# A three-part fp32 network on one core: the sequence transform folded a second time, its sums taken after the output projection, and the layer norm of two blocks inverted by token

## The chip, the cores and the metric

The kernel runs on one core of one Trainium2 chip. The metric is device time in microseconds; lower is better. A core has five engines with queues of their own: TensorE (PE in the views, with its weight loads, LDWEIGHTS, shown apart as PEld), VectorE (DVE), ScalarE (ACT), GpSimd (POOL) and SyncE (SP), which here issues DMAs.

## The reference

Three blocks follow one another, on 8 batches of 576 tokens with 512 features.

```python
# attention with random features, 8 heads of 64
q_p, k_p = phi(q), phi(k)          # phi: x @ w_phi, minus the row's largest |.|, exp(+) and exp(-)
num = q_p @ (k_p^T v);  den = q_p . sum(k_p) + 1e-6;  x = num / den
# gated mixer: 5 causal taps along the sequence
gate = sigmoid(sum_k conv_w[k] * x shifted by 4-k)
x = (gate * (x @ w_val)) @ w_out
# Fourier mixer and MLP
mixed = real(fft(fft(x, axis=sequence), axis=features))
u = x + mixed
un = (u - mean(u)) / sqrt(var(u) + 1e-6)
out = u + relu(un @ w_ch1) @ w_ch2
```

## The kernel before

**Numbers.** All products of the mixer, the transforms and the MLP are in fp32 split in two: a high part (copied to the fp32r type, on ACT: `o_hi`) and the rest (`o_lo`, on DVE or POOL), and three matmuls, high x high, high x low, low x high (`mm3`). The Fourier transforms are products with tables of cosines and sines.

**Stages.** Attention runs in 48 hand-written steps. Then a "mix" stage does, for each batch b, these parts, each written as a list of operations: `note_x` (load x, split it into `xh`), `note_taps` (the gate, sums in `acc`), `note_V` (value projection `val<-xh,wv`, 12 matmuls for each of 4 feature chunks and 2 halves of the sequence; the gate's product; the split `ge`), `note_W` (output projection `ps<-ge,wo`, also 8 times 12 matmuls; results in `x2`, which the trace calls x), `note_FD` (transform over features, `ps<-ft,f`, results `Y` and the rest `rem`), `note_SD` (transform over the sequence, `ps<-sq,Y` and `ps<-sr,rem`, and the sum `u`, stored to DRAM). Between them stand the first two half blocks of the layer norm (`ln_first`) and sums of MLP weights on POOL (`note_sums`). The MLP follows, in five blocks of tokens, with seven products where eight would be plain.

**Folding.** A real sequence has a transform that is symmetric, so one works on sums and differences of token s and token 576 - s. Before, these are taken of the gated value, ahead of W (`gs<-gv,val`): halves of 290 columns (289 tokens and one that overlaps) go through W as an even and an odd part, a = 0 and 1. The features are folded in the same way by the order of `w_out`'s columns and by `fs` (c and c - 2). In SD the results of 290 columns are added to x2, and `u` is made of its even and odd part, forwards and, read backwards, for the other half of the sequence. Feature 256 goes its own way, on single rows: `xr` into FD, `c256`, `r256`, and a product with 97 weight columns at the end of each four batches.

**Order.** After the parts are noted, `place_ops` sets the order of every engine in one list. It has a cost for each operation (by engine and columns), works backwards from the end to a due time for each, shifts some due times by a table of hand-made numbers (`MOVES`, operation number: half microseconds), and then lets each engine take the ready operation that is due first. An operation marked "vp" goes to DVE or POOL, whichever the list finds sooner. Engines then run in that order and wait by semaphores. `MOVES` and the noted order of V and W in `note_mix` are what the change touches here.

Nearly all instructions of this stage stand in the trace at one line (64 before, 66 after), that of a helper that issues them, so groups go by the names of their tiles.

## Time and profile before

| | |
|---|---|
| median of three runs | 1301.6 us (1301.53 to 1302.43) |
| profiled execution | 1302.1 us, span 1300.3 us |
| TensorE busy | 1281.4 us, 99% of the span |
| DVE, ACT, POOL busy | 1130.3, 917.2, 786.9 us |
| granted TensorE clock, mean | 0.999 of full speed |

The attention takes about the first 300 us of the span, the mix stage lies from there to about 585, the MLP from about 585 to 1296. Busy time counts instructions at work; a busy TensorE may still be at a lower clock, which the column PEclk of the windows shows as a share of full speed.

### The profile page before, as it was taken

The page shows a single profiled execution, that of the slowest core. Times are in us where ns is not written, and L with a number is a line of the kernel's source. Part 1 is how long each engine was busy: PE and PEld are TensorE (multiplying, and loading weights), DVE is VectorE, ACT ScalarE, POOL GpSimd, SP SyncE. Part 2 cuts the span into 40 slices and gives each one's busy share as a digit, 9 for nine tenths or more (in the row PEclk, how much of TensorE's full clock was granted, in tenths as well). Part 3 has the DMA queues.
Part 4 walks back from the last instruction along what each step waited for, and adds up shares of the span by engine and source line. Part 5 has one row for each costly group of instructions (what it writes and reads, how often), then busy time and mean ns, then how long its engine had stood idle before and what let it go on. Part 6 is the DMA issues. An engine that isn't in the chain of part 4 may idle for free.

```text
span 1300.3 us, 30757 instructions
## 1 busy us (share of the span) xinstructions
PE 1281.4 (99%) x11952; PEld 1181.0 (91%) x11952; DVE 1130.3 (87%) x1773; ACT 917.2 (71%) x1719; POOL 786.9 (61%) x660
## 2 busy tenths in 40 slices
PE   8999999999999999999999999999999999999998
PEld 7899999998999999998888888888888888899997
DVE  6888888888999999698889988898989898888785
...
GB/s 309 200 289 319 326 298 289 172 120 96 118 187 138 139 160 130 170 60 295 111 99 100 276 104 104 104 185 197 105 100 134 245 107 103 102 165 162 109 82 90
DMA packets 147005, 214.62 MB, mean 165 GB/s; under 512 B 18854, under 2 KB 105382, under 8 KB 146860
## 3 DMA queue, kind: packets, MB, share of 16 engines
...
HBM read 165.63 MB, written 46.99 MB: 164 GB/s over the span
## 4 chain that ended last, share of the span: by engine, by line
PE 86%; ACT 5%; DMA 4%; DVE 4%; issue 0%; POOL 0%; SPq 0%; POOLq 0%; DVEq 0%; ACTq 0%
PE x L64 15%; PE cx L64 15%; PE cy L64 11%; PE ps L64 11%; PE y L64 8%; PE val L64 7%; PE kv L64 5%; PE pj L64 4%; PE nm L64 4%; PE z L64 4%; PE yt L314 2%; PE xt L352 1%; DMA r<-s_scr 1%; ACT qe L64 1%; DMA x<-u_scr 1%; DVE acc L64 1%
## 5 line engine op out<-in xcount | busy, mean ns | idle before, releaser
L64 POOL TENSOR_TENSOR r<-r 128x256 fp32r<-128x256 f32 (+1 forms) x305 | 296.7, 990 | 246.7 <-ACT r L64 226.9
L64 ACT ACTIVATE r<-r 128x256 fp32r<-128x256 f32 (+1 forms) x420 | 195.6, 488 | 57.5 <-DMA r<-s_scr 50.5
L64 PE MATMUL x<-un,r 128*128 128x462 f32 (+1 forms) x960 | 221.3, 372 | 1.0 <-ACT r L64 0.9
L64 PE MATMUL cx<-h,r 128*128 128x462 f32 (+1 forms) x960 | 213.8, 371 | 1.0 <-DVE acc L64 1.0
L64 PEld LDWEIGHTS x<-un,r 128*128 128x128 f32 x960 | 180.3, 188 | 22.6 <-ACT r L64 1.2
L64 PEld LDWEIGHTS cx<-h,r 128*128 128x128 f32 x960 | 180.3, 188 | 22.0 <-DVE acc L64 1.8
L64 PE MATMUL cy<-h,r 128*128 128x462 f32 (+1 forms) x720 | 159.9, 370 | 0.0
L64 PEld LDWEIGHTS cy<-h,r 128*128 128x128 f32 x720 | 135.3, 188 | 15.0
L64 PE MATMUL val<-xh,wv 128*128 128x290 f32 x768 | 115.2, 301 | 2.9 <-DVE xh L64 2.0
L64 PE MATMUL y<-un,r 128*128 128x462 f32 (+1 forms) x480 | 114.0, 372 | 1.1 <-DVE h L64 1.0
L64 PEld LDWEIGHTS val<-xh,wv 128*128 128x128 f32 x768 | 107.5, 191 | 4.1 <-DVE xh L64 2.2
L64 PE MATMUL ps<-ge,wo 128*128 128x290 f32 x768 | 107.5, 297 | 0.0
L270 DVE TENSOR_REDUCE m<-pj 128x6 f32<-128x768 f32 x96 | 91.5, 953 | 15.5 <-PE pj L64 14.8
L64 PEld LDWEIGHTS ps<-ge,wo 128*128 128x128 f32 x768 | 104.3, 189 | 0.4 <-DVE x L64 0.2
L64 PEld LDWEIGHTS y<-un,r 128*128 128x128 f32 x480 | 89.8, 188 | 12.4 <-DVE h L64 2.2
L64 DVE TENSOR_TENSOR acc<-cx,acc 128x924 f32<-128x924 f32 (+1 forms) x80 | 88.9, 1112 | 13.5 <-PE cx L64 10.4
L271 DVE TENSOR_TENSOR y<-pj,m 128x768 f32<-128x768 f32 x96 | 92.0, 958 | 6.9 <-DVE m L270 0.5
L64 DVE SCALAR_TENSOR_TENSOR acc<-xf,cw,acc 128x576 f32<-128x576 f32 x112 | 91.2, 814 | 4.4 <-ACT acc L64 3.8
L64 PE MATMUL kv<-vraw,ke 128*64 128x66 f32 x2560 | 87.6, 224 | 1.9 <-ACT kvT L64 1.7
L64 ACT ACTIVATE qe<-yt 128x768 f32<-128x768 f32 x96 | 72.5, 810 | 23.9 <-PE yt L314 23.8
L64 ACT ACTIVATE h<-z 128x462 fp32r<-128x462 f32 (+1 forms) x120 | 66.3, 552 | 28.2 <-DVE z L64 24.4
L64 PE MATMUL pj<-wp,kqraw 64*128 64x128 f32 x1152 | 80.7, 287 | 5.5 <-DMA kqraw<-in_k_dram 4.6
(175 smaller groups left out, 2741.2 us busy)
## 6 DMA issues: line engine op xcount, KB each, us to landing
...
r<-s_scr SPq DMA_DIRECT2D x140, 256.0 KB, 2.6
...
```

The source lines that it names most:

```text
L64: return lambda *a, **k: f(*(resolve(x) for x in a), **{n: resolve(x) for n, x in k.items()})
L270: nc.vector.tensor_reduce(out=m, in_=pv, axis=AX.X, op=ALU.max, apply_absolute_value=True)
L271: nc.vector.tensor_tensor(out=y, in0=pv, in1=m.unsqueeze(3).to_broadcast([128, 2, CH, F]), op=ALU.subtract)
L314: nc.tensor.transpose(t[:, h, j * F:(j + 1) * F], y[:, h, j, :], ident)
L352: nc.tensor.transpose(t[:, 0, j * F:(j + 1) * F], x[:, j].rearrange("p h d -> p (h d)"), ident)
```

## The change

**V** now works on plain halves of 288 tokens and does not fold: the gated value is split as it is. **W** does the same, in halves of 288 columns. **The folds** come after W, on the projected output: `fs` is the sum and the difference of feature chunks c - 2 and c (eight operations a batch, two for each half), `first_fold` folds it about token 288, `fold` folds that again about token 144 into `fe`, even columns for sums and odd ones for differences, and `parted` splits it into high and low, in a part of 256 and a part of 33 columns that is written three times (99). These folds may go to DVE or POOL. Row 256 is folded on one partition by POOL (`xe`). **FD** has 99 instead of 33 weight columns in its third part. **SD**: for each half of the features and each a, one product of `sr,rem` over 292 columns opens both halves of a bank, and six products of `sq,Y` over 146 columns follow, where each parity of the output needs only one parity of the input. Even and odd columns lie apart in PSUM and are read interleaved (`by_parity`): ACT copies the result for a = 1, DVE adds and subtracts the one for a = 0 (`fs<-ps,fs`), and four `u` operations of 576 columns add it to x2. **The layer norm's** first two half blocks sum squares with the tokens as weight columns (`inverse_by_token`), take the root and the inverse of four columns a token chunk, and spread them again by transposes; the MLP's other blocks keep the old way. Tables are loaded as eight pieces instead of twelve and scaled on the way. `note_mix` notes V and W in another order, `MOVES` is new (some 140 entries for about 50), and `PINS` fixes the engine of 22 operations.

```diff
-        gv, gs = later(("gv", i)), later(("gs", i))
+        gv = later(("gs", i))
         for n in range(2):
-            p = later(("pv", n))
-            sl = slice(0, NE) if n == 0 else slice(S - NE, S)
+            p = later(("pv", n))[:, 0:HS]
+            sl = slice(HS * n, HS * n + HS)
 
...
-                        mm3(p[:, 0:NE], (wv[0][:, c, ws], wv[1][:, c, ws]), (h[:, c, sl], l[:, c, sl]), c == 0, c == 3)
+                        mm3(p, (wv[0][:, c, ws], wv[1][:, c, ws]), (h[:, c, sl], l[:, c, sl]), c == 0, c == 3)
...
-            o_tt("v", (gv, p[:, 0:NE])[n], p[:, 0:NE], gate[:, sl], ALU.mult, NE, [("pv", n), ("sg", i)], [(("gv", i), ("pv", n))[n]])
-        p = later(("pv", 1))
-        op("v", 1, lambda e: vec.tensor_copy(out=p[:, NE:NE + 1], in_=gv[:, 0:1]), [("gv", i), ("pv", 1)], [("pv", 1)])
-        for a, alu in ((0, ALU.add), (1, ALU.subtract)):
-            o_tt("v", gs[:, a], gv, p[:, NE:0:-1], alu, NE, [("gv", i), ("pv", 1)], [("gs", i, a)])
+            o_tt("v", gv[:, sl], p, gate[:, sl], ALU.mult, HS, [("pv", n), ("sg", i)], [("gs", i, n)])
...
+        o_lo("vp", gl, gv, gh, S, gk + [("ge", g, m, 0)], [("ge", g, m, 1)] + [("done", "g", m)] * (b == NB - 1 and m >= 2))
...
     def seq_pass(p, main, rem, a):
+        mm(p, rem, sr[0:3 * NR, a].rearrange("p e k -> p (e k)"), start=True, stop=False, skip_group_check=True)
         for j in range(2):
-            mm3(p, main(j), (sq[:, 2 * j, a], sq[:, 2 * j + 1, a]), j == 0, False)
-        if a == 0:
-            mm(p, rem, sr[:, 0], start=False, stop=False)
-            mm(p, rem, sr[:, 1], start=False, stop=True)
-        else:
-            mm(p, rem, sr[:, 2], start=False, stop=True)
-
...
+            e = j ^ a
+            (h, l), o = main(j), p[:, NP * e:NP * e + NP]
+            for m, (w, x) in enumerate(((h, 0), (h, 1), (l, 0))):
+                mm(o, w, sq[:, x, a, e], start=False, stop=m == 2, skip_group_check=True)
+
+    def by_parity(p):
+        return p.rearrange("p (e k) -> p k e", e=2)[:, 0:NE // 2]
+
+    def pairs(t):
+        return t.rearrange("p (k e) -> p k e", e=2)
+
+    SD_TIME = 6 * 0.071 + 0.134
+
+    def fold(e, dst, src, keys, out):
+        n = HS // 2
+        for i, alu in ((0, ALU.add), (1, ALU.subtract)):
+            o_tt(e, dst[:, :, i:HS:2], src[:, :, 0:n], src[:, :, HS:n:-1], alu, (1 if out[0] == "xe" else 2) * n, keys, [out + (i,)])
+        op("a", 0, lambda e: hi_act(dst[:, :, HS:HS + 1], src[:, :, n:n + 1]), keys, [out + (2,)], 0.2)
+        return [out + (i,) for i in range(3)]
+
+    def first_fold(e, dst, src, keys, alu, out):
+        o_tt(e, dst[:, 1:HS], src[:, 1:HS], src[:, S - 1:HS:-1], alu, HS - 1, keys, out)
+
+    def parted(e, high, low, src, keys, out):
+        a = 2 if out[0] == "f" else 1
+        cols = [lambda v: v[:, :, 0:256].rearrange("p a (k e) -> p a e k", e=2)]
+        cols.append(lambda v: v[:, :, 256:HS + 1].unsqueeze(2).to_broadcast([v.shape[0], v.shape[1], 3, NR]))
+        to = [lambda v: v[:, :, 0:256].rearrange("p a (e k) -> p a e k", e=2)]
+        to.append(lambda v: v[:, :, 256:256 + 3 * NR].rearrange("p a (t r) -> p a t r", r=NR))
+        for i in range(2):
+            n = (256, 3 * NR)[i] * a
+            o_hi(to[i](high), Late(lambda i=i: cols[i](resolve(src))), n, keys, [out + (0, i)])
+            o_lo(e, to[i](low), Late(lambda i=i: cols[i](resolve(src))), to[i](high), n, keys + [out + (0, i)], [out + (1, i)])
+
+    T_LO = "vp"
...
+    def inverse_by_token(sh, sl, keys, bank):
+        rs, at, m = later("rs"), (0, 116, 232, HB - 116), 116
+        b, p = bank()
+
+        def var(e, p=p):
+            for i, z in enumerate(at):
+                for x in (sh, sl):
+                    mm(p[0:m, 2 * i:2 * i + 2], x[:, z:z + m], ones[:, 0:2], start=x is sh, stop=x is sl)
+        op("m", 0, var, keys, [b], 8 * 0.065)
+        o_act(rs[0:m], p[0:m, 0:8:2], ACTF.Sqrt, 4, [b], ["rs"], bias=eps[0:m])
+        op("v", 0, lambda e: vec.reciprocal(out=rs[0:m], in_=rs[0:m]), ["rs"], ["rs"], 0.11)
+        b, p = bank()
+
+        def spread(e):
+            for i, z in enumerate(at):
+                pe.transpose(p[:, z:z + m], rs[0:m, i:i + 1].to_broadcast([m, 128]), ident[0:m, 0:m])
+        op("m", 0, spread, ["rs"], [b], 4 * 0.11)
+        return b, p
...
+        if tokens:
+            b, p = inverse_by_token(sh, sl, [hk, lk], bank)
+            p = p[:, 0:n]
...
-            o_tt("v", x, x, s1.unsqueeze(1).to_broadcast([128, 2, n]), ALU.mult, 2 * n, ["s1", ak[c]], [ak[c]])
+            o_tt("v", x, x, p.unsqueeze(1).to_broadcast([128, 2, n]), ALU.mult, 2 * n, [b, ak[c]], [ak[c]])
...
-        for a in range(2):
+        for n in range(2):
             k, p = next(ring)
...
+            sl = slice(HS * n, HS * n + HS)
...
-                    mm3(p, (wo[0][:, kk, ws], wo[1][:, kk, ws]), (gh[:, kk, a], gl[:, kk, a]), kk == 0, kk == 3)
+                    mm3(p, (wo[0][:, kk, ws], wo[1][:, kk, ws]), (gh[:, kk, sl], gl[:, kk, sl]), kk == 0, kk == 3)
...
             if c >= 2:
-                o_tt("v", fs[:, a], t[:, c - 2, a], p, (ALU.add, ALU.subtract)[a], NE, [k, ("x2", w, c - 2, a)], [("fs", a)])
+                for a in range(2):
+                    o_tt("v", fs[:, a, sl], t[:, c - 2, sl], p, (ALU.add, ALU.subtract)[a], HS, [k, ("x2", w, c - 2, n)], [("fs", a, n)])
...
         if c >= 2:
             c0 = c - 2
-            fk = [("fs", 0), ("fs", 1)]
-            o_hi(f[0][:, c0], fs, 2 * NE, fk, [("f", c0, 0)])
-            o_lo(K["t_lo"], f[1][:, c0], fs, f[0][:, c0], 2 * NE, fk + [("f", c0, 0)], [("f", c0, 1)])
+            fe = tl["fe"]
+            sk = [("fs", a, n) for a in range(2) for n in range(2)]
+            for a in range(2):
+                first_fold("vp", fs[:, a], fs[:, a], sk[2 * a:2 * a + 2], (ALU.add, ALU.subtract)[a], sk[2 * a:2 * a + 2])
+            fk = fold("vp", fe, fs, sk, ("fe",))
+            parted(K["t_lo"], f[0][:, c0], f[1][:, c0], fe, fk, ("f", c0))
         if c == 2:
...
+            r, xe = later("xr"), later("xe")
+            tk = [("x2", w, 2, n) for n in range(2)]
+            op("a", 0, lambda e: hi_act(xe[:, 0, 0:HS + 1:HS], t[0:1, 2, 0:HS + 1:HS]), tk, ["xe0"], 0.2)
+            first_fold("p", xe[:, 0], t[0:1, 2], tk, ALU.add, ["xe1"])
+            parted("v", r[0:1].unsqueeze(1), r[32:33].unsqueeze(1), xe[:, 1:2], fold("p", xe[:, 1:2], xe[:, 0:1], ["xe0", "xe1"], ("xe",)), ("xr",))
...
-            n = 128 if j < 2 else 33
+            n = 128 if j < 2 else 3 * NR
...
+                    r, rk = later(("rem", a))[0:n], ("rem", a)
+                    p = p[0:n]
+                    o_hi(r, p, NL, [k], [rk])
+                    op("v", NL, lambda e, r=r, p=p: vec.scalar_tensor_tensor(
+                        out=r, in0=f32(r), scalar=marks[0:3 * NR, 0:1], in1=p, op0=ALU.mult, op1=ALU.add
+                    ), [k, rk], [rk])
...
+            banks = [next(ring) for a in range(2)]
+            for a in (1, 0):
+                k, p = banks[a]
+                p = p[:, 0:2 * NP]
                 rem = later(("rem", a))
 
...
-                if a == 0:
-                    o_tt("v", t[:, i::2, 0, :], t[:, i::2, 0, :], p.unsqueeze(1).to_broadcast([128, 2, NE]), ALU.add, 2 * NE,
-                         [k, ("x2", w, i, 0), ("x2", w, i + 2, 0)], [("x2", w, i, 0), ("x2", w, i + 2, 0)])
+                    seq_pass(p, lambda j: (yh[:, j, a, ls], yl[:, j, a, ls]), rem[0:3 * NR, ls], a)
+                yk = [("Y", j, a, h) for j in range(2) for h in range(2)] + [("rem", a)]
+                op("m", 0, prod, yk, [k], SD_TIME)
+                if a:
+                    o_act(pairs(pm[:, 0]), by_parity(p), ACTF.Copy, NE, [k], PM[0])
                 else:
-                    for c, alu in ((i, ALU.subtract), (i + 2, ALU.add)):
-                        o_tt("v", t[:, c, 1], t[:, c, 1], p, alu, NE, [k, ("x2", w, c, 1)], [("x2", w, c, 1)])
-        for i in range(2):
+                    for j, alu in ((1, ALU.add), (0, ALU.subtract)):
+                        o_tt("v", pairs(pm[:, j]), by_parity(p), pairs(pm[:, 0]), alu, NE, [k] + PM[0], PM[j])
             cs = slice(i, 4, 2)
-            ek = [("x2", w, c, a) for c in (i, i + 2) for a in range(2)]
-            o_tt(K["uf"], u[:, cs, 0:HS + 1], t[:, cs, 0, 0:HS + 1], t[:, cs, 1, 0:HS + 1], ALU.add, 2 * HS + 2, ek, [("u", i, 0)])
-            o_tt(K["uf"], u[:, cs, HS + 1:S], t[:, cs, 0, HS - 1:0:-1], t[:, cs, 1, HS - 1:0:-1], ALU.subtract, 2 * HS - 2, ek, [("u", i, 1)] + ["mixed"] * w)
+            for n in range(2):
+                sl = slice(HS * n, HS * n + HS)
+                x = pm[:, ::-1, HS:0:-1] if n else pm[:, :, 0:HS]
+                o_tt(K["uf"], u[:, cs, sl], t[:, cs, sl], x, ALU.add, S, PM[0] + PM[1] + [("x2", w, c, n) for c in (i, i + 2)], [("u", i, n)] + ["mixed"] * (w * n))
...
-            for i, c in enumerate((0, 2, 1, 3)):
-                if i < 3:
+            turn = iter(SUMS[b])
+            for what, i in (("W", 0), ("V", 0), ("W", 2), ("V", 1), ("W", 1), ("W", 3), ("V", 2), ("V", 3)):
+                if what == "V":
                     note_taps(b + 1, i)
                     note_V(b + 1, i)
-                note_W(b, c)
-                add_sums(SUMS[b][i])
-            add_sums(SUMS[b][4])
-            note_taps(b + 1, 3)
-            note_V(b + 1, 3)
+                else:
+                    note_W(b, i)
+                    add_sums(next(turn))
+            add_sums(next(turn))
...
+        11: 15, 21: -164, 48: -22, 132: 117, 139: 20, 173: 45, 184: -274, 197: -52, 242: 4, 246: -17, 250: -46,
...
+    PINS = {
+        75: "p", 175: "p", 249: "v", 260: "v", 448: "v", 498: "v", 585: "p", 732: "p", 828: "p", 833: "v", 873: "p",```

What the order of instructions becomes at three places follows. A row is a line number, the operation, output and inputs with the number of their tile, partitions by columns, and how many such stand in a row.

First TensorE, where the first sequence transform (batch 0) starts. Before:

```order
L64 MATMUL ps_5797<-sq,Y_5783 128x290 x2
L64 MATMUL ps_5797<-sq,Y_5788 128x290
L64 MATMUL ps_5797<-sq,Y_5783 128x290 x2
L64 MATMUL ps_5797<-sq,Y_5788 128x290
L64 MATMUL ps_5797<-sr,rem_5785 128x290 x2
L64 MATMUL ps_5798<-sq,Y_5783 128x290 x2
L64 MATMUL ps_5798<-sq,Y_5788 128x290
```

TensorE at the same place after:

```order
L66 MATMUL ps_5771<-sr,rem_5762 128x292
L66 MATMUL ps_5771<-sq,Y_5757 128x146 x2
L66 MATMUL ps_5771<-sq,Y_5761 128x146
L66 MATMUL ps_5771<-sq,Y_5757 128x146 x2
L66 MATMUL ps_5771<-sq,Y_5761 128x146
L66 MATMUL ps_5768<-sr,rem_5758 128x292
```

The rest's product has moved to the front, its second one for a = 0 is gone, and the six others have half the columns.

Second TensorE, at the passage from batch 0's value projection to batch 1, with the last transposes of the attention (`xt`). Before, sixteen rows of `val` of batch 1 (24 products) stand between the last `xt` and the first W; these are the last eleven of them and W:

```order
L64 MATMUL val_5463<-xh,wv_119 128x290
L64 MATMUL val_5463<-xh,wv_118 128x290 x2
L64 MATMUL val_5463<-xh,wv_119 128x290
L64 MATMUL val_5460<-xh,wv_118 128x290 x2
L64 MATMUL val_5460<-xh,wv_119 128x290
L64 MATMUL val_5463<-xh,wv_118 128x290 x2
L64 MATMUL val_5463<-xh,wv_119 128x290
L64 MATMUL val_5460<-xh,wv_118 128x290 x2
L64 MATMUL val_5460<-xh,wv_119 128x290
L64 MATMUL val_5463<-xh,wv_118 128x290 x2
L64 MATMUL val_5463<-xh,wv_119 128x290
L64 MATMUL ps_5795<-ge,wo 128x290 x12
```

TensorE at the same place after, from the attention's last `nm` products on:

```order
L66 MATMUL nm<-kvT,qe 64x65 x24
L355 MATMUL xt<-ident,xs 128x128 x3
L66 MATMUL val_5467<-xh,wv_119 128x288 x2
L66 MATMUL val_5467<-xh,wv_120 128x288
L66 MATMUL val_5467<-xh,wv_119 128x288 x2
L66 MATMUL val_5467<-xh,wv_120 128x288
L66 MATMUL val_5469<-xh,wv_119 128x288 x2
L66 MATMUL val_5469<-xh,wv_120 128x288
L66 MATMUL val_5469<-xh,wv_119 128x288 x2
L66 MATMUL val_5469<-xh,wv_120 128x288
L355 MATMUL xt<-ident,xs 128x128 x3
L66 MATMUL ps_5768<-ge,wo 128x288 x12
```

Only the first two of the four parts of each half (12 products) are left ahead of W, `nm` and `xt` have come down among them, and two more W blocks of 12 follow before the next `val`.

Third DVE, where W of batch 0 brings chunks 2 and 3, beside the taps (`acc`) of batch 1. Before:

```order
L64 TENSOR_TENSOR gv<-val_5460,acc 128x290
L64 SCALAR_TENSOR_TENSOR acc<-xf,cw,acc 128x2x288
L64 TENSOR_TENSOR fs<-x_5778,ps_5797 128x290
L64 SCALAR_TENSOR_TENSOR acc<-xf,cw,acc 128x2x288
L64 TENSOR_TENSOR xr_5784<-ps_5797,xr_5784 1x290
L64 SCALAR_TENSOR_TENSOR acc<-xf,cw,acc 128x2x288
L64 TENSOR_TENSOR val_5463<-val_5463,acc 128x290
L64 SCALAR_TENSOR_TENSOR acc<-xf,cw,acc 128x2x288
L64 COPY val_5463<-gv 128x1
L64 TENSOR_TENSOR gs<-gv,val_5463 128x290 x2
L64 TENSOR_TENSOR gv<-val_5460,acc 128x290
L64 TENSOR_TENSOR fs<-x_5778,ps_5798 128x290
```

DVE at the same place after:

```order
L66 TENSOR_TENSOR gs<-val_5467,acc 128x288
L66 SCALAR_TENSOR_TENSOR acc<-xf,cw,acc 128x2x288
L66 TENSOR_TENSOR fe<-fs 128x2x144 x2
L66 TENSOR_TENSOR fs<-x_5750,ps_5771 128x288 x2
L66 TENSOR_TENSOR f_5760<-fe,f_5756 128x2x256
L66 TENSOR_TENSOR fs<-x_5750,ps_5771 128x288 x2
L66 TENSOR_TENSOR gs<-val_5469,acc 128x288
L66 TENSOR_TENSOR fs<-fs 128x287 x2
L66 TENSOR_TENSOR gs<-val_5467,acc 128x288
L66 TENSOR_TENSOR fe<-fs 128x2x144
L66 TENSOR_TENSOR xr<-xe,xr 1x256
```

The two folds of `gv` and the copy are gone from the value's side, and on the output's side `fs` is done twice as often and followed by `fs<-fs`, `fe<-fs` and a split `f<-fe`. Over the whole kernel DVE has 1775 instructions before and 1778 after, ACT 1737 and 1800, POOL 665 and 690, TensorE 8946 and 8948.

## Rows read from the trace of the kernel before

**Rows 1.** The page's first part: busy time, share of the span, instructions of each engine.

```profile
PE 1281.4 (99%) x11952; PEld 1181.0 (91%) x11952; DVE 1130.3 (87%) x1773; ACT 917.2 (71%) x1719; POOL 786.9 (61%) x660
```

**Rows 2.** Windows: length; busy PE, PEld, DVE, ACT, POOL; PEclk, DMA share, GB/s.

```profile
310.00:517.00 207.00, 205.96 (x1534) 204.27 (x1535) 196.02 (x368) 121.74 (x245) 138.07 (x129) 0.99 0.41 140
...
585.00:1295.70 710.70, 707.53 (x3371) 632.45 (x3369) 620.04 (x896) 500.31 (x1035) 409.99 (x385) 1.00 0.45 140
```

**Rows 3.** The chain that ended last: start, length, engine and tile, matmuls in it.

```profile
285.44 0.66 PE yt L314 x6
...
534.29 11.27 PE ps L64 x84
...
597.10 2.51 PE x L64 x12
```

**Rows 4.** Weight loads by shape: count, busy us, mean ns, idle before.

```profile
L64 PEld LDWEIGHTS ps<-sq,Y 128*128 128x128 f32 x192 | 27.5, 189 | 0.1
...
L64 PEld LDWEIGHTS ps<-ft,f 128*33 128x33 f32 x96 | 10.4, 109 | 0.9
L64 PEld LDWEIGHTS ps<-sq,c 128*97 128x97 f32 x12 | 1.6, 162 | 0.5 <-DVE Y L64 0.5
```

**Rows 5.** Timeline of the weight loads, pairs: start, first start to last end.

```profile
395.82 0.30 PEld L64 LDWEIGHTS ps<-ge,wo 128*128 128x128 f32 x2 [0.15 <-DVE x L64]
...
524.52 0.14 PEld L64 LDWEIGHTS ps<-ft,f 128*33 128x33 f32 x2
...
578.76 0.25 PEld L64 LDWEIGHTS ps<-sq,c 128*97 128x97 f32 x2 [0.47 <-DVE Y L64]
```

**Rows 6.** Timeline of PE at the passage to batch 1, idle before in brackets.

```profile
310.40 4.90 PE L64 MATMUL val<-xh,wv 128*128 128x290 f32 x23 [1.99 <-DVE xh L64]
```

**Rows 7.** Windows behind that stop, columns as in rows 2.

```profile
310.40:313.80 3.40, 3.40 (x14) 3.37 (x15) 3.36 (x7) 0.86 (x2) 2.63 (x3) 0.50 0.15 58
313.80:316.90 3.10, 3.10 (x25) 3.10 (x25) 2.79 (x7) 0.71 (x2) 1.45 (x3) 1.00 0.21 74
```

**Rows 8.** Timeline of DVE there.

```profile
308.36 1.98 DVE L64 TENSOR_TENSOR xh<-xf,xh 128x576 fp32r<-128x576 f32 x1
...
311.53 0.74 DVE L64 TENSOR_TENSOR xh<-xf,xh 128x576 fp32r<-128x576 f32 x1
```

**Rows 9.** Timeline of POOL there.

```profile
308.33 3.30 POOL L64 TENSOR_TENSOR xh<-xf,xh 128x576 fp32r<-128x576 f32 x2 [1.67 <-ACT xh L64]
```

**Rows 10.** DVE by shape, whole run: busy us, mean ns, idle before.

```profile
L64 DVE TENSOR_TENSOR r<-r 128x512 fp32r<-128x512 f32 x46 | 34.5, 753 | 9.6 <-ACT r L64 9.4
...
L64 DVE TENSOR_TENSOR r<-r 128x256 fp32r<-128x256 f32 x69 | 30.2, 441 | 2.4 <-ACT r L64 2.3
...
L64 DVE TENSOR_TENSOR gs<-gv,val 128x290 f32<-128x290 f32 x64 | 26.4, 450 | 0.7
L64 DVE RECIPROCAL x<-x 128x116 f32<-128x116 f32 x30 | 26.0, 867 | 1.1 <-ACT x L64 1.1
...
L64 DVE TENSOR_TENSOR fs<-x,ps 128x290 f32<-128x290 f32 x28 | 12.5, 450 | 9.1 <-PE ps L64 8.7 <-ACT xr L64 0.2
L64 DVE TENSOR_TENSOR x<-x,ps 128x290 f32<-128x290 f32 x28 | 11.4, 446 | 0.0
L64 DVE TENSOR_TENSOR xh<-xf,xh 128x576 fp32r<-128x576 f32 x12 | 11.2, 944 | 0.0
L64 DVE TENSOR_TENSOR x<-x,ps 128x580 f32<-128x580 f32 x14 | 10.5, 752 | 0.4 <-PE ps L64 0.3
...
L64 DVE TENSOR_TENSOR ge<-gs,ge 128x580 fp32r<-128x580 f32 x12 | 10.1, 840 | 0.3
...
L64 DVE COPY val<-gv 128x1 f32<-128x1 f32 x32 | 4.9, 155 | 0.3
L64 DVE TENSOR_TENSOR u<-x 128x574 f32<-128x574 f32 x5 | 4.8, 955 | 0.0
```

**Rows 11.** ACT by shape: the high part of the gated value.

```profile
L64 ACT ACTIVATE ge<-gs 128x580 fp32r<-128x580 f32 x32 | 21.8, 682 | 10.5 <-DVE gs L64 10.5
```

170 lines of the change are left out of this document (95 added, 75 removed), and 22 rows, old and new, of tables (MOVES, STAGES).

## The prediction

> **What bounds it now.** I read the page's first part, then windows of the mix stage, then TensorE by shape, and last the waits. TensorE is busy for 1281.4 of the 1300.3 us span [rows 1]. So time is gained only by giving it less work or less waiting, and lost only where another engine makes it wait. The window 310 to 517 us, where one batch's gate and value projection overlap the output projection of the batch before and the transforms, shows how near that other engine is: PE 205.96 of 207.00 us, DVE 196.02, POOL 138.07, ACT 121.74 [rows 2]. DVE has 11.0 us in hand there, and almost everything that this change adds outside TensorE lands on it. In the MLP PE stands idle for 3.2 of 710.7 us [rows 2]; nothing in the diff edits that part, though its order is laid anew.
>
> What a product costs follows from runs in the chain: 84 products of 290 columns take 11.27 us, 134 ns each, 12 of 462 columns take 2.51 us, 209 ns each [rows 3]. That is 0.436 ns a column, and would give a 146-column product 71 ns. But six transposes of 128 columns take 0.66 us, 110 ns each [rows 3], far above the line. They load 128 weight columns each; and in pairs of loads the second starts 0.30 - 0.189 = 0.11 us after the first for 128 columns, 0.25 - 0.162 = 0.09 for 97, 0.14 - 0.109 = 0.03 for 33 [rows 4, 5]. A narrow product is thus paced by its weights. The diff charges 0.071 us for a 146-column product; I take 0.110.
>
> **The change, TensorE.** Sequence transform: before, each batch has 30 products of 290 columns (8 and 7 for the two values of a, twice), 4.02 us; after, four groups of one of 292 (0.135) and six of 146 with 128 weight columns, 4 x (0.135 + 6 x 0.110) = 3.18. That is -0.84 a batch, -6.7 in eight; by the bound of the line it would be 2.24, -14.2 in eight. The product for row 256, done twice with 97 weight columns, falls from 8 x 0.134 = 1.07 to 0.135 + 6 x 0.09 = 0.68: -0.8. V and W lose 2 columns in each of 1536 products: 1536 x 2 x 0.436 ns = -1.3. The third part of the feature transform goes from 33 to 99 weight columns; its load of about 0.09 stays below the 0.12 that its 258 columns take, so 0. Layer norm by token: two products of 462 (0.42) become eight with 116 weight columns (between 0.09 and 0.11, I take 0.10) and four transposes (0.11): +0.82, twice, +1.6. Sum: -7.2, of which -5.0 lies in 310 to 517 (six batches' transforms, V and W, one row 256, both norms).
>
> **The stall at the transition.** At 308.40 PE stands for 1.99 us before the first value product of batch 1, for DVE's split xh [rows 6]. That split took 1.98 us against 0.74 for the same one three microseconds later [rows 8]; POOL was at two xh splits from 308.33 for 3.30 us [rows 9]. After the stop the granted clock is 0.50, that is the 1.2 GHz level: 14 products in 3.40 us, where the next 3.10 us hold 25 at 1.00 [rows 7]; at that pace the 14 take 1.7, so 1.7 us more are lost. Before, all 24 products of the first value block come ahead of W, so all four splits are due at once. After, only 12 (the first two splits) come ahead, with 24 `nm` products and the transposes before them, and then three W blocks, 36 x 0.134 = 4.8 us, in which the other splits may land. What W itself waits for, the last `ge` of batch 0, is a DVE gate (0.450), an ACT copy (0.682) and a split (0.840) [rows 10, 11] after the last value product, with hand-overs some 2.3 us; six transposes and 12 products alone are 0.66 + 1.6 = 2.3, and the 24 `nm` products come on top. So the stall of 2.0 and the lapse of 1.7 can both go. Bounds 0 (a new stop there as long) and -3.7; I take -2.5, since the splits get no shorter and DVE and POOL still do them side by side.
>
> **DVE, and what it gives back.** Removed: 64 folds of the gated value 26.4, 32 one-column copies 4.9, the combine of the sequence transform 11.4 + 10.5 and 3.3 for its last batch, 11 u of 0.955 = 10.5, eight reciprocals 6.9 [rows 10], and some 8 of smaller rows (1 x 290 and 97-row pieces at 0.45 as the other 290s, three splits that POOL takes over): 82. Added, each by the row nearest in shape [rows 10]: 32 `fs<-x,ps` of 288 and 32 `fs<-ps,fs` of 290 at 0.450, 28.8; 20 folds of 287 and 27 of 2x144 at 0.450, 21.2; 10 splits of 2x256 at 0.753 and 3 of 198 at about 0.35, 8.6; 16 `xr`, 256 long at 0.441 or 99 long at about 0.2, 5.1; 26 u of 576 at 0.955, 24.8; four of 97 rows, 1.8. That is 90, +8 in all. PSUM is now read with a stride of 146 in `fs<-ps,fs`; no row has that, and the old fold that read `val` backwards took 0.450 like a plain one, so I price it the same. Six of eight batches lie in 310 to 517, and all eight reciprocals: 0.75 x (8 + 6.9) - 6.9 = +4.3. DVE then has 200.3 us of work there, and PE 205.96 - 5.0, about 201. The 11 us in hand are down to under 1. An engine that feeds and is fed does not run without gaps: part of its idle time was waits for PE (`fs<-x,ps` alone shows 9.1 us of it in the whole run [rows 10]), which need not go. I keep a third of the 11 us: DVE wants 204, and gives back 3.5 to PE. Bounds: 0, and all 11, which is +10.
>
> ACT gets about 80 instructions more, of which 16 copies of 290 columns; with 121.74 of 207 busy it hides them. POOL takes 12 to 16 first folds and the one-partition folds for fifteen of the longer u, about even, with 138.07 of 207 busy. The table pieces fall in the attention, where they are a few copies; 0. The MLP's order is shifted: 0, with 3.2 us of idle at stake either way by about 1.
>
> Sum: -7.2 - 2.5 + 3.5 = -6.2. Against the profiled execution's 1302.1 (span 1300.3 and 1.8 around it) that is 1295.9; the median 1301.6 lies 0.5 below it, so **1295**.
>
> **Rivals.** First, DVE becomes the bound, and the kernel is slower. The order has 91 more DVE instructions that read two SBUF tiles (20 and 27 folds, 13 splits, 16 `xr`, 15 u), 68 in six batches. The xh split, which reads two as well, means 0.944 over twelve [rows 10] and 0.74 at its best [rows 8], 0.20 more when POOL is at such work, 1.24 more at worst. At 0.20 each, 13.6 us are added: DVE wants 214 in that stretch and, with 3.5 of gaps, 217.5, 10.5 more than now; the two batches outside still save 2.2, so 1310, and 1304 to 1310 for part of it, 1306 as its middle. It decides from 0.09 a piece on: there the 6.2 are gone. The Trainium skill, "SBUF — State Buffer", "Who interferes with whom", states the mechanism: a DVE instruction with two SBUF inputs shares a read port with a GpSimd instruction that reads SBUF, and the one that comes second is blocked for the whole of the other. By that rule each added fold may be hit; the trace agrees in the one split of 1.98 us beside POOL's. Against the rival: POOL is busy two thirds of the time already and the DVE splits now mean only 0.20 over their best. Chance 0.18.
>
> Second, the narrow products run at the line's 71 ns: TensorE loses 7.5 us more. In 310 to 517 PE would want 195 and DVE still 204, so most of that is not cashed: 1292, and 1287 if DVE runs without gaps. Chance 0.08. The Trainium skill, "TensorE: Matmul & The Clock Gate", "Back-to-back issue gap", gives N/2.4 + 2.5 ns for a lone product, 63 ns at 146 columns, and a sustained 81 ns at 128; by the first the change would gain about 9 us more on TensorE, by the second 5. The transposes at 110 and the loads 0.11 apart disagree with both.
>
> Third, the gain is eaten: PE is relieved as above, but DVE keeps all its gaps (200.3 + 11 = 211, 4 more than now) or half of them, or the stall comes back elsewhere. 1299 to 1304. Chance 0.14.
>
> **Numbers.** The forecast has 0.60, with 1291 to 1298.5 as its own range (stall -3.7 and no gaps; stall 0, gaps 3.5). A measurement of this kernel tells about 0.2%, 2.6 us, from no change: under 1299.0 is faster, over 1304.2 slower. Faster 0.60 + 0.08 = 0.68, same 0.14, slower 0.18. The range goes from 1287 (second rival) to 1305, beyond which most of the first rival lies.
>
> **What would show it.** In the new trace: the 146-column products 110 ns apart with loads 189 ns long; no stop of PE near 308 and no clock of 0.50 behind it; DVE's busy time near 200 of 204 us in the six middle batches, with PE's waits there going to DVE's `fs`, `fe` and `f`; u at 0.955, folds at 0.45. Folds at 0.65 or more beside POOL's would be the first rival; PE waits for `f` after W, where the two folds now stand between W and the feature transform, would make the forecast too low.

## The result and the profile after

The changed kernel takes 1313.4 us (median of five runs, 1309.3 to 1315.0) where the kernel before took 1301.6 beside it (1297.9 to 1302.5). The ratio is 1.0087 with a 95% interval of 1.0063 to 1.0111: slower, by about 11 us. The forecast was 1295, and 1305 the end of its range. Of the cases on record the first rival, DVE as the bound, comes nearest, and 1313 lies beyond that too.

The profiled execution took 1314.1 us, 1312.3 of them its span. The first line of its page, to be held against [rows 1]:

```profile
PE 1280.4 (98%) x11954; PEld 1177.8 (90%) x11954; DVE 1145.1 (87%) x1776; ACT 930.7 (71%) x1782; POOL 795.5 (61%) x685
```

TensorE is busy 1.0 us less than before and the span is 12.0 us longer, so PE stands idle 13.0 us more. DVE has 14.8 us more of busy time, where the forecast had 8. The windows (columns as in [rows 2]) of the middle batches, of the worst stretch in them (with one window of 1 us inside it), and of the start of the MLP:

```profile
310.00:525.00 215.00, 204.36 (x1536) 201.02 (x1536) 196.83 (x347) 130.63 (x291) 142.70 (x146) 0.98 0.40 138
...
476.00:480.00 4.00, 2.45 (x12) 2.10 (x12) 3.91 (x9) 2.83 (x6) 1.16 (x2) 0.72 0.35 141
...
478.00:479.00 1.00, 1.00 (x6) 0.92 (x4) 0.99 (x3) 1.00 (x3) 0.00 (x0) 0.50 0.00 0
...
480.00:484.00 4.00, 1.50 (x6) 1.53 (x7) 4.00 (x6) 1.79 (x4) 3.84 (x5) 0.50 0.00 0
484.00:488.00 4.00, 4.00 (x20) 4.00 (x19) 3.71 (x4) 1.95 (x4) 4.00 (x4) 0.50 0.00 0
...
590.00:610.00 20.00, 15.43 (x70) 13.13 (x70) 17.29 (x31) 12.79 (x28) 7.26 (x6) 0.91 0.59 193
```

The same 215 us of the kernel before read:

```profile
310.00:525.00 215.00, 213.96 (x1596) 212.15 (x1597) 202.22 (x380) 126.07 (x256) 141.41 (x132) 0.99 0.41 140
```

PE was idle for 1.0 of these 215 us before and is for 10.6 now. DVE has not become busier: 202.2 before, 196.8 now, some 13 and 18 us idle. The mean over the stage thus shows no bound; the two rows of 476 to 484 do: DVE is busy for 7.91 of 8 us there, while PE waits for 4.05.

The stops of PE, in its timeline (start, length, idle before with its releaser):

```profile
309.32 1.87 PE L66 MATMUL ps<-ge,wo 128*128 128x288 f32 x12 [0.58 <-ACT xT L66]
...
362.06 6.62 PE L66 MATMUL val<-xh,wv 128*128 128x288 f32 x48 [1.29 <-DVE gs L66]
373.25 1.66 PE L66 MATMUL ps<-ft,f 128*99 128x258 f32 x12 [1.44 <-DVE Y L66]
...
476.82 2.45 PE L66 MATMUL val<-xh,wv 128*128 128x288 f32 x12 [2.11 <-DVE gs L66]
482.50 3.22 PE L66 MATMUL val<-xh,wv 128*128 128x288 f32 x12 [3.23 <-DVE gs L66]
...
592.13 2.74 PE L66 MATMUL x<-un,r 128*128 128x462 f32 x12 [1.02 <-DVE fs L66]
598.46 1.53 PE L66 MATMUL x<-un,r 128*128 128x462 f32 x6 [2.33 <-DVE c L66]
601.21 2.68 PE L66 MATMUL x<-un,r 128*128 128x462 f32 x6 [1.23 <-ACT c L66]
```

The two stops before 476.82 and 482.50 end with a gated value `gs`, which frees the PSUM bank that the next value product wants. DVE in the stretch ahead of them:

```profile
471.35 1.74 DVE L66 TENSOR_TENSOR fs<-fs 128x287 f32<-128x287 f32 x1
...
477.28 0.45 DVE L66 TENSOR_TENSOR fs<-fs 128x287 f32<-128x287 f32 x1
...
478.19 0.83 DVE L66 TENSOR_TENSOR fe<-fs 128x288 f32<-128x288 f32 x2
...
479.31 1.95 DVE L66 TENSOR_TENSOR xh<-xf,xh 128x576 fp32r<-128x576 f32 x1
481.19 0.81 DVE L66 SCALAR_TENSOR_TENSOR acc<-xf,cw,acc 128x576 f32<-128x576 f32 x1
481.91 0.45 DVE L66 TENSOR_TENSOR gs<-val,acc 128x288 f32<-128x288 f32 x1
```

and POOL beside it:

```profile
471.36 1.41 POOL L66 TENSOR_TENSOR ge<-gs,ge 128x576 fp32r<-128x576 f32 x1
...
479.25 1.40 POOL L66 TENSOR_TENSOR xh<-xf,xh 128x576 fp32r<-128x576 f32 x1 [2.84 <-ACT xh L66]
```

The gate that PE waits for takes 0.45 us. It stands in line behind the folds of W's output and a split, and two of these pieces, begun within a tenth of a microsecond of a POOL instruction, take 1.74 and 1.95 us where the same shapes take 0.45 and 0.74 ([rows 8], and the fold at 477.28). That is the mechanism of [rows 8, 9], now with folds in it. Behind the stop of 2.11 us the granted clock falls to 0.50, the 1.2 GHz level: the window of 478 to 479 has it already, ahead of the second stop. It stays there through the stop of 3.23 us and until 488; about 0.28 x 2.45 + 0.50 x 5.50 = 3.4 us of TensorE's time are lost to it. Behind the stops of 1.29 and 1.44 us at 362 and 373 no window of 4 us shows less than 0.99.

By stage (from the first value product to the last of the sequence transform, then to the last product; own sums over the trace) the two kernels compare so: the mix takes 301.7 us after 293.3, with 11.9 of PE idle after 3.1; the MLP 716.3 after 712.8, with 7.5 idle after 3.1. Some 2.8 us of the MLP's products lie in the mix now. Counted where they belong, the mix is 5.6 us longer than before and the MLP 6.3, so the start of the MLP holds half of the 12 us by which the span grew.

### The profile page after: what moved, and what is told of

It reads as the page before. It is cut to its first block, busy times and chain, and to the rows that moved or that the text cites. A ratio compares the mean times of both kernels' runs of the same rounds, so it can differ in the third digit from the quotient of the medians.

```text
span 1312.3 us, 30886 instructions
## 1 busy us (share of the span) xinstructions
PE 1280.4 (98%) x11954; PEld 1177.8 (90%) x11954; DVE 1145.1 (87%) x1776; ACT 930.7 (71%) x1782; POOL 795.5 (61%) x685
## 4 chain that ended last, share of the span: by engine, by line
PE 53%; DVE 6%; ACT 2%; DMA 2%; issue 1%; POOL 0%; SPq 0%; ACTq 0%; DVEq 0%
PE cx L66 14%; PE x L66 13%; PE cy L66 10%; PE y L66 7%; PE ps L66 4%; PE z L66 4%; DMA r<-s_scr 2%; DVE acc L66 2%; PE val L66 1%; DVE fs L66 1%; DVE h L66 1%; ACT r L66 0%; ACT h L66 0%; DVE B L66 0%; ACT c L66 0%
## 5 line engine op out<-in xcount | busy, mean ns | idle before, releaser
L66 POOL TENSOR_TENSOR r<-r 128x256 fp32r<-128x256 f32 (+1 forms) x307 | 302.3, 1001 | 257.4 <-ACT r L66 239.0
L66 ACT ACTIVATE r<-r 128x256 fp32r<-128x256 f32 (+1 forms) x420 | 195.9, 489 | 50.6 <-DMA r<-s_scr 45.2
L66 PE MATMUL x<-un,r 128*128 128x462 f32 (+1 forms) x960 | 223.1, 373 | 5.3 <-DVE c L66 2.3
L66 PE MATMUL cx<-h,r 128*128 128x462 f32 (+1 forms) x960 | 214.1, 371 | 1.0 <-DVE acc L66 1.0
L66 PEld LDWEIGHTS x<-un,r 128*128 128x128 f32 x960 | 180.8, 189 | 27.7 <-DVE c L66 3.6
L66 PEld LDWEIGHTS cx<-h,r 128*128 128x128 f32 x960 | 180.3, 188 | 22.0 <-DVE acc L66 1.8
L66 PE MATMUL cy<-h,r 128*128 128x462 f32 (+1 forms) x720 | 160.2, 371 | 0.0
L66 PEld LDWEIGHTS cy<-h,r 128*128 128x128 f32 x720 | 135.4, 188 | 15.2
L66 PE MATMUL val<-xh,wv 128*128 128x288 f32 x768 | 115.3, 301 | 8.7 <-DVE gs L66 8.4
L66 PEld LDWEIGHTS val<-xh,wv 128*128 128x128 f32 x768 | 106.5, 191 | 11.5 <-DVE gs L66 6.9
L66 PE MATMUL y<-un,r 128*128 128x462 f32 (+1 forms) x480 | 114.1, 372 | 1.2 <-DVE h L66 1.2
L66 PE MATMUL ps<-ge,wo 128*128 128x288 f32 x768 | 107.0, 296 | 0.8 <-ACT xT L66 0.6
L273 DVE TENSOR_REDUCE m<-pj 128x6 f32<-128x768 f32 x96 | 91.5, 953 | 15.6 <-PE pj L66 14.0
L66 PEld LDWEIGHTS ps<-ge,wo 128*128 128x128 f32 x768 | 103.1, 188 | 1.6 <-ACT xT L66 0.8
L66 PEld LDWEIGHTS y<-un,r 128*128 128x128 f32 x480 | 90.3, 189 | 12.5 <-DVE h L66 2.0
L66 DVE TENSOR_TENSOR acc<-cx,acc 128x924 f32<-128x924 f32 (+1 forms) x80 | 88.9, 1112 | 12.2 <-PE cx L66 10.2
L66 DVE SCALAR_TENSOR_TENSOR acc<-xf,cw,acc 128x576 f32<-128x576 f32 x112 | 91.2, 814 | 1.8 <-ACT acc L66 1.1
L66 ACT ACTIVATE h<-z 128x462 fp32r<-128x462 f32 (+1 forms) x120 | 66.4, 554 | 33.7 <-DVE z L66 28.4
L66 ACT ACTIVATE qe<-yt 128x768 f32<-128x768 f32 x96 | 72.6, 812 | 23.4 <-PE yt L317 23.4
L66 PE MATMUL kv<-vraw,ke 128*64 128x66 f32 x2560 | 87.8, 224 | 0.8 <-ACT kvT L66 0.5
L66 PE MATMUL pj<-wp,kqraw 64*128 64x128 f32 x1152 | 81.0, 287 | 6.4 <-DMA kqraw<-in_k_dram 4.8
```

Source lines behind the costliest of these rows:

```text
L66: return lambda *a, **k: f(*(resolve(x) for x in a), **{n: resolve(x) for n, x in k.items()})
L273: nc.vector.tensor_reduce(out=m, in_=pv, axis=AX.X, op=ALU.max, apply_absolute_value=True)
```

## The experiments

The theory after this reading: DVE sets the pace of the mix; it has more to do than was priced, and pieces that begin together with POOL's are two to four times as long, so gates come late. Rivals: the loss is one of the particular order, which the new due times made, and another order would get it back; the clock or the MLP's start make most of it, and DVE little. The kernels leave work out, move it or split it, and nothing else; the kernel before, run beside each of them, had medians of 1301.2 to 1302.9. In the expectations theory A is DVE's load, B its waits beside POOL, C the order.

**POOL made quiet.** POOL's splits, sums and folds from batch 1 on, up to the last batch's W, work on 8 columns instead of their own width. POOL's part of that work is left out; DVE's stays.

```diff
+    def short(e, *t):
+        t = [resolve(x) for x in t]
+        if e == "p":
+            t = [x[(slice(None),) * (len(x.shape) - 1) + (slice(0, 8),)] for x in t]
+        return t
```

> The changed kernel, every engine's order kept, but POOL's tensor operations of the mix stage (splits, folds, sums of MLP weights) work on 8 columns instead of all from batch 1 on; what they leave out is not computed. Theory A (load: DVE has more work, keeps its old gaps, and sets the pace): folds shorten by 0.2 us each and the stops of TensorE in the mix stage, 11.9 us now, fall by less than half; 1307 to 1311. Theory B (port: the added two-input operations are held up by POOL): fs<-fs and fe<-fs fall from 0.65 and 0.61 to 0.45 and the stops to under 4 us; 1299 to 1303. Theory C (order: the instructions stand in an unlucky order, whatever their length): stops stay where they are; 1310 to 1314.

Measured 1304.2 us, ratio 1.0016 (0.9997 to 1.0034): 9.2 us of the changed kernel's loss are gone, a time between the ranges of theories A and B. DVE does the same instructions, by shape (busy us, mean ns); first the changed kernel, then this one:

```profile
L66 DVE TENSOR_TENSOR u<-x,fs 128x576 f32<-128x576 f32 x22 | 16.9, 788 | 0.1
L66 DVE TENSOR_TENSOR fe<-fs 128x288 f32<-128x288 f32 x27 | 15.6, 612 | 0.3
L66 DVE TENSOR_TENSOR fs<-ps,fs 128x290 f32<-128x290 f32 x32 | 14.6, 455 | 2.7 <-PE ps L66 1.5 <-ACT fs L66 1.0
L66 DVE TENSOR_TENSOR fs<-fs 128x287 f32<-128x287 f32 x20 | 12.7, 654 | 0.1
L66 DVE TENSOR_TENSOR xh<-xf,xh 128x576 fp32r<-128x576 f32 x11 | 11.6, 1057 | 0.0
...
L66 DVE TENSOR_TENSOR xr<-xe,xr 1x99 fp32r<-1x99 f32 x8 | 2.6, 320 | 0.2
L66 DVE TENSOR_TENSOR f<-fe,f 128x198 fp32r<-128x198 f32 x3 | 2.2, 744 | 0.2 <-issue 0.2
```

```profile
L66 DVE TENSOR_TENSOR u<-x,fs 128x576 f32<-128x576 f32 x22 | 16.7, 782 | 0.1
...
L66 DVE TENSOR_TENSOR fe<-fs 128x288 f32<-128x288 f32 x27 | 12.5, 497 | 0.3
L66 DVE TENSOR_TENSOR fs<-fs 128x287 f32<-128x287 f32 x20 | 9.2, 482 | 0.1
L66 DVE TENSOR_TENSOR xh<-xf,xh 128x576 fp32r<-128x576 f32 x11 | 8.7, 787 | 0.0
```

The folds cost 0.14 us more for each (3.1 and 3.5 us over 47), and the splits `xh` 0.27, with POOL at its whole work beside them. Not every piece with two SBUF inputs does: `u` hardly changes, and the 10 splits `f` of 512 columns take 0.690 in both. The kernel also gains by POOL's results coming earlier, and this run does not separate the two. The two stops of 2.11 and 3.23 us are 0.82 and 2.65 us here; the second is now named for ACT's part of `xh`:

```profile
474.98 2.79 PE L66 MATMUL val<-xh,wv 128*128 128x288 f32 x12 [2.65 <-ACT xh L66]
...
474.38 0.45 DVE L66 TENSOR_TENSOR gs<-val,acc 128x288 f32<-128x288 f32 x1
```

DVE's gate ends at 474.83, 0.12 us before ACT's part. DVE works without a gap from 470.35 to there on nine pieces, none of them long (the split takes 0.76, the folds about 0.45 each). So DVE's line alone, with no collision in it, makes a stop of some 2.5 us at this place.

**The same quiet in the kernel before.** The same edit, on the kernel before.

> The kernel before, order kept, POOL's tensor operations of the mix stage on 8 columns from batch 1 on as in quiet_pool; what they leave out is not computed. If the port's cost is new with the change (theory B as a cause of the loss): the kernel before gains little, 1299 to 1301.5, against the 9 us that the changed one gained. If both suffer alike, 1292 to 1295, and the port explains no difference.

Measured 1299.5, ratio 0.999 (0.9977 to 1.0004). It gains 2.6 us by the medians, which the interval does not tell from nothing, where the changed kernel gains 9.2. PE's idle time in the mix is the same as without the edit, 3.0 us after 3.1; the stop near 310 is there (2.00 us), and what is missing is the lower clock behind it. So POOL's work costs the changed kernel some 6.6 us that it does not cost the one before. How much of that is longer pieces, and how much POOL's results coming late, is not shown.

**Short folds.** The folds of W's output (`fs<-fs`, `fe<-fs`) and those of row 256 work on 8 columns from batch 1 on, on DVE and POOL; the rest of the folded columns is not computed.

```diff
+            if cut:
+                t = [v[(slice(None),) * (len(v.shape) - 1) + (slice(0, 8),)] for v in t]
```

> The changed kernel, every engine's order kept, but first_fold and fold (fs<-fs, fe<-fs, xe) work on 8 columns from batch 1 on, on DVE and POOL alike; the rest of the folds is not computed. Some 20 us of DVE time leave the mix stage. Theory A (load): the stops between 360 and 530 us and the lower clock behind them go, only those at the MLP's start stay in part; 1297 to 1302. Theory B (port): the collisions go with the folds; the same 1297 to 1302, with xh down from 1.06 to about 0.9. Theory C (order): 1308 to 1313.

Measured 1304.0, ratio 1.0008 (0.9993 to 1.0023), 9.5 less than the changed kernel and above the range of theories A and B. DVE's busy time falls by 19.0 us (1145.1 to 1126.1), the time by half of that. POOL's falls by 17.9 (795.5 to 777.6), since it does a part of the folds, so this run does not separate the two engines either. In 310 to 525 this run and the quiet one have the same DVE busy time to the hundredth, 191.35, and nearly the same for PE:

```profile
310.00:525.00 215.00, 209.20 (x1591) 206.43 (x1592) 191.35 (x359) 133.31 (x304) 134.32 (x151) 0.99 0.41 141
```

Neither is a version to keep, since both leave work out; and neither comes below the kernel before, though each frees DVE of more than the 14.8 us that the change added.

**Layer norm as before.** The four operations of the inverse by token keep their places, but the sum goes to 462 columns by two products, and DVE inverts 462 columns of 128 rows in four reciprocals; the spreading transposes are left out. The rest of the change stays.

```diff
-                    mm(p[0:m, 2 * i:2 * i + 2], x[:, z:z + m], ones[:, 0:2], start=x is sh, stop=x is sl)
+                mm(p[:, 0:HB], ones, x, start=x is sh, stop=x is sl)
...
+            for z in range(0, HB, 116):
+                x = s1[:, z:min(HB, z + 116)]
+                vec.reciprocal(out=x, in_=x)
```

> The changed kernel, order kept, with the first two half blocks of the layer norm inverted in the old way at the same places (two products of 462, a root of 462 columns, four reciprocals of 0.86 on DVE, no transposes). DVE gets 6.6 us more in two bursts, TensorE 1.2 us less. Theory A (load): slower than the changed kernel by 3 to 6 us, 1316 to 1319, with new stops of TensorE near the two bursts. Theories B and C: the bursts fall into gaps, within 2 us of the changed kernel, 1311 to 1315.

Measured 1319.3, ratio 1.0121 (1.0092 to 1.0151): 5.8 us slower than the changed kernel, as theory A had it, though PE is spared the norm's small products; no run of the one overlaps a run of the other. DVE's busy time is up by 4.5, ACT's by 2.6 (its roots are 462 columns wide here). The gates come later still, in the waits of PE from 300 to 620 us (total, times, longest), first of the changed kernel:

```profile
PE val L66 <- DVE gs L66: 8.4, 7, 3.2
PE x L66 <- DVE c L66: 2.3, 1, 2.3
```

```profile
PE val L66 <- DVE gs L66: 10.0, 7, 3.8
PE ps L66 <- DVE fs L66: 2.9, 2, 2.2
PE ps L66 <- ACT fs L66: 2.4, 1, 2.4
```

So work that is taken from PE and given to DVE, with a little to ACT, makes this kernel slower, and the waits that grow are mostly DVE's: DVE bounds the stage. Of the experiments this one adds to DVE without touching POOL's work. It also says that the one part of the change that relieves DVE pays.

**Another order.** Only the tables of due times and of fixed engines are replaced, by others with 137 and 47 entries; every instruction stays.

```diff
     MOVES = {
-        11: 15, 21: -164, 48: -22, 132: 117, 139: 20, 173: 45, 184: -274, 197: -52, 242: 4, 246: -17, 250: -46,
...
+        15: -128, 16: -87, 17: -27, 27: 7, 40: 353, 47: 20, 61: -188, 112: 47, 132: 385, 148: -215, 164: 87, 181: 225,
```

> The changed kernel with the same instructions in another order: a new table MOVES of 137 entries and 47 PINS, looked for with the true 0.795 us of a sequence product group in place of 0.56. Theory C (order): the same work without the stops at 477, 482 and 592 us; below 1300. Theory A (load): DVE has as much to do and TensorE waits for it elsewhere; 1304 to 1310, with 8 us or more of stops left from 300 us on.

Measured 1314.3, ratio 1.0098 (1.0079 to 1.0118), the same as the changed kernel, and outside the ranges of theories A (1304 to 1310) and C (below 1300). Its stops lie in part elsewhere (2.39 us at 363, 3.38 at 482, 4.3 in sum from 590 to 599) and add up to 12.6 in the mix. No lower clock follows either of the two long ones:

```profile
482.45 2.97 PE L66 MATMUL val<-xh,wv 128*128 128x288 f32 x18 [3.38 <-ACT f L66]
...
482.00:486.00 4.00, 3.48 (x25) 3.27 (x26) 3.93 (x7) 2.34 (x5) 3.46 (x4) 1.00 0.00 0
```

One other order is no proof that none is better, but the loss is not that of the one order in the table.

**The last batch's folds short.** In the last batch the four `fs<-ps,fs` and the four `u` work on 8 columns, to see whether they make the stops at the start of the MLP; that batch's output is left out.

```diff
+            if w:
+                t = [v[:, 0:4] if len(v.shape) == 3 and v.shape[2] == 2 else v[:, :, 0:8] for v in t]
```

> The changed kernel, order kept, with the last batch's four fs<-ps,fs and four u of the sequence transform on 8 columns; the rest of them is not computed. 4 to 5 us of DVE leave the place where the MLP begins. Theory A (load): of the stops at 592, 598 and 601 us (4.6 us) and the lower clock behind them most go; 1307 to 1310. Theory C (order): the MLP's own operations stand behind other things; within 2 us of the changed kernel, 1311 to 1315.

Measured 1310.3, ratio 1.0064 (1.0039 to 1.0089): 3.1 us less by the medians, but the two intervals overlap. By the traces the MLP takes 714.0 us after 716.3, so a part of its start, about 2.3 us, hangs on them; two stops there stay (1.28 us for `c` of DVE, 1.98 for `c` of ACT).

The trace shows something else as well. Up to the last batch this kernel has the same instructions as the changed one, and still its mix takes 298.3 us after 301.7. The stop of 3.23 us is one of 1.34 here, and the split ahead of the gate takes 0.76 where it took 1.95:

```profile
477.66 0.76 DVE L66 TENSOR_TENSOR xh<-xf,xh 128x576 fp32r<-128x576 f32 x1
...
477.68 2.01 POOL L66 TENSOR_TENSOR xh<-xf,xh 128x576 fp32r<-128x576 f32 x1 [2.92 <-ACT xh L66]
...
479.66 2.06 PE L66 MATMUL val<-xh,wv 128*128 128x288 f32 x12 [1.34 <-DVE gs L66]
```

Here DVE's split began 0.02 us ahead of POOL's and POOL's is the long one; in the changed kernel it began 0.06 us behind. The changed kernel's worst stop is thus that of one execution, and some 3 us of what a single trace shows there change from one execution to the next.

**POOL's instructions in parts.** If a DVE instruction waits for a whole POOL instruction, shorter POOL instructions should cost less. Those of 400 columns or more are issued in two parts, or four, in the whole program; then in two only before the MLP; then in two in the kernel before. Nothing is left out.

```diff
+    def in_parts(f, cols, *t):
+        t = [resolve(x) for x in t]
+        n = t[0].shape[-1]
+        k = 2 if cols >= 400 and n % 2 == 0 else 1
+        for j in range(k):
+            at = (slice(None),) * (len(t[0].shape) - 1) + (slice(j * n // k, (j + 1) * n // k),)
+            f(*(x[at] for x in t))
```

> The changed kernel, order kept, each tensor operation of POOL of 400 columns or more issued as two of half the columns; all is computed. POOL's work grows by about 0.15 us for each. Theory B (port, held for a whole instruction): a DVE fold beside POOL's split waits half as long; fs<-fs and fe<-fs means fall from 0.65 and 0.61 to about 0.55, the split of 1.95 us near 479 to about 1.3; 1306 to 1310. If it is only the amount of POOL's traffic that slows DVE, means stay and the time is 1312 to 1316, POOL's additions being the only effect. Theory A (load) says no more than what B gives back.

> As halves, with four parts: DVE waits a quarter as long, means near 0.50; POOL's work grows by 0.45 us an operation, some 40 us in the mix stage of its 108 us in hand. Theory B: 1303 to 1309, less if POOL's own results come late. If not the port: 1312 to 1320.

> As halves, but in the mix stage alone: all is computed. Theory B: the mix stage ends 4 to 5 us sooner than in the changed kernel, as it did in halves, and the MLP loses nothing; 1306 to 1310.

> The kernel before with the same halving of POOL's operations. Theory B: its own stop of 1.99 us at 310 us comes from a DVE split that waits for POOL's; halved, the stop falls to about 1.2 us and the lower clock behind it goes; 1298 to 1300. Otherwise 1301 to 1303.

Halves: 1310.2, ratio 1.0068 (1.0046 to 1.0089), 3.2 less than the changed kernel, with intervals that overlap. Quarters: 1323.1, ratio 1.0161 (1.0132 to 1.0191), 9.7 more, by the traces all of it in the MLP (726.1 us). Halves before the MLP alone: 1312.6, ratio 1.0081 (1.0066 to 1.0096). Halves in the kernel before: 1309.8, ratio 1.0065 (1.0041 to 1.009), 8.6 slower than without, where a gain was expected; its stop at 312 is down to 1.39 us, but the lower clock behind it is still there, and stops of 1.35 and 1.83 stand further on. DVE by shape in the first of these:

```profile
L66 DVE TENSOR_TENSOR fe<-fs 128x288 f32<-128x288 f32 x27 | 15.5, 606 | 0.3
L66 DVE TENSOR_TENSOR fs<-fs 128x287 f32<-128x287 f32 x20 | 12.1, 625 | 0.1
L66 DVE TENSOR_TENSOR xh<-xf,xh 128x576 fp32r<-128x576 f32 x11 | 9.6, 873 | 0.0
```

The splits `xh` get shorter, 1.057 to 0.873; the folds stay near where they were, at 0.606 and 0.625, and `u` gets longer, 0.788 to 0.867. The expected 0.55 for a fold did not come. POOL pays for the parts with 40.2 us of busy time in the whole run, and the MLP takes 719.1 us after 716.3; that its splits come late there would fit, but was not tested. To halve before the MLP alone should then have been the best of both, and brought 0.9, less than the runs of the changed kernel differ among each other. This line was inconclusive.

**All at once.** Quiet POOL, short folds and the short last batch together; all that those three leave out is left out.

> The changed kernel, order kept, with quiet_pool, short_folds and short_last together. Theories A and B (DVE's load, part of it waiting for POOL): with both gone TensorE's own gain of 7 to 8 us shows, 1291 to 1297, mix-stage stops under 3 us. Theory C (order): stops of 2 to 3 us near 477 stay with the lower clock behind them, and 2 us or more at the MLP's start; 1299 to 1304.

Measured 1300.4, ratio 0.9991 (0.9981 to 1.0): 13.0 less than the changed kernel and no better than the kernel before. Theories A and B had 1291 to 1297, theory C 1299 to 1304, so by the time alone the order would have it. By the stages it is not the mix that fails A and B: that takes 288.0 us now, 5.3 less than in the kernel before, near the 6.2 that the forecast had for the whole, with 3.8 of PE idle where under 3 were expected. But the MLP takes 715.8, 3.0 more. PE at its start, ACT beside it, and the windows there:

```profile
583.53 1.53 PE L66 MATMUL x<-un,r 128*128 128x462 f32 x6 [1.28 <-DVE c L66]
...
588.37 2.68 PE L66 MATMUL x<-un,r 128*128 128x462 f32 x6 [3.31 <-ACT c L66]
```

```profile
586.53 0.42 ACT L66 ACTIVATE r<-r 128x256 fp32r<-128x256 f32 x1 [2.41 <-DMA r<-s_scr]
```

```profile
580.00:590.00 10.00, 5.41 (x21) 4.19 (x20) 5.89 (x13) 5.48 (x12) 1.79 (x4) 0.81 0.91 304
590.00:600.00 10.00, 10.00 (x42) 8.83 (x42) 7.52 (x14) 8.06 (x17) 2.02 (x3) 0.85 1.06 371
```

ACT stands 2.41 us for a transfer of the MLP's weights (`r<-s_scr`) with the copy `c` that PE wants in line behind it, at a DMA share of 0.91 to 1.06. In the trace of the changed kernel ACT has no wait for a transfer between 584 and 604; the wait stands only in this kernel, which comes to the place some 13 us sooner. It was not tested by itself.

## Why the prediction was wrong, step by step

**TensorE's work: right.** The 146-column products start 111 ns apart (median), as taken, not 71; in the weight loads by shape the 128-column load is 0.191 us long, as before:

```profile
L66 PE MATMUL ps<-sq,Y 128*128 128x146 f32 x192 | 25.3, 268 | 0.0
L66 PEld LDWEIGHTS ps<-sq,Y 128*128 128x128 f32 x192 | 24.8, 191 | 0.0
```

In the mix, idle time excluded (own sums), the sequence transform falls by 6.8 us (forecast 6.7), the product for row 256 by 0.95 (0.8), W by 0.5 (0.7), the two norms add 1.2 (1.6). The second rival, narrow products at the line's price, is out. The Trainium skill's "TensorE: Matmul & The Clock Gate", "Back-to-back issue gap", weighed there, gave 63 ns for a lone product of this width and 81 ns sustained at 128 columns; the rows agree with neither.

**The stall at the transition: right.** W starts at 309.3 instead of 315.1, behind an idle time of 0.58 us (the timeline above), and no lower clock follows. That is the 1.99 us and the lapse of [rows 6, 7] less the new 0.58, some 3.1, where 2.5 was taken.

**DVE, and what it gives back: wrong, and this is the step that failed.** "I keep a third of the 11 us: DVE wants 204, and gives back 3.5 to PE." (By its own 204 and 201 that is 3.0, and the 5.0 taken off PE there is 4.8 by its own terms; neither matters.) The mix is 8.4 us longer, 2.8 of them the MLP's products; with the 7.2 and 2.5 taken off for TensorE and the stall, the term of 3.5 came to some 15. Two things are off in it. The smaller: the work added to DVE was sized at 8 us and came to 14.8. Folds were priced at 0.45 and took 0.612 and 0.654 (+8.5 over 47), the splits `f` of 198 took 0.744 against 0.35, `xr` of 99 columns 0.320 against 0.2; `u` at 0.788 against 0.955 gave 3.7 of that back. The price was the row nearest in shape, but one with PSUM for one input; with two SBUF inputs a fold is slower by 0.14 and a split `xh` by 0.27 beside POOL (quiet POOL). The rival had this, at 0.20 each and "from 0.09 a piece on". It held against itself that the splits had a mean only 0.20 over their best, and had that very 0.20 as its price. It also put that price on `u`, which the quiet run does not show.

The larger: the gaps of DVE. The forecast let DVE close up to two thirds of them. It closed none; DVE is idle for 18 of 215 us where it was for 13, and PE's idle time in the mix went from 3.1 to 11.9, not up by 3.5, though the stop of 1.99 is gone. The engines work through one order without skipping ahead: when a gate is late PE stops, and what PE would have made for DVE in that time is late in its turn. That last link, from PE's stop back to DVE's idle time, is argued from the fixed order and was not tested. A sum of busy times over 215 us cannot show this, since DVE at 92% of a stage bounds it for 3 us here and 5 there and waits in between. The third rival had the gaps kept and the first the pieces longer, each alone; both came true together. The experiments bear out that the mix hangs on DVE's line: 1319.3 with more for DVE, 1313.4 as it is, 1304 with either POOL's work or the folds taken out, 1300.4 with both and the last batch's pieces. How the loss divides between DVE's own load and POOL's work beside it they do not show, since the folds are POOL's in part.

**The MLP's start, priced at 0 with about 1 us either way: wrong.** It lost 6.3 us, a third of the 18 between the forecast and the span. Its stops come to 4.6 us (592, 598 and 601), and the window of 590 to 610 shows 0.91 for the clock. The three stops stand at the same products, about as long, in the reordered kernel (1.06, 2.07 and 1.16). The forecast excluded it because the diff edits nothing there; but the stage begins where DVE ends the last batch's combine, and to cut that (the short last batch) took 2.3 us out of this stage by the traces. What makes the rest is not shown.

**What the forecast did not have at all** is the clock within the mix, 3.4 us. It fell behind a stop of 2.11 us and came back at 488. A stop does not always bring it: none fell behind the 2.39 and 3.38 us of the reordered kernel, nor behind the 2.00 of the kernel before with POOL quiet.

Open: how much of quiet POOL's 9 us is shorter DVE pieces, and how much POOL's own results being earlier; what makes the MLP's start slow beyond the last batch's pieces; and whether an order exists that avoids the loss, of which one other was tried. No version was found that beats the kernel before.
